# A fused attention and MLP training step: stage 1's weights in seven pieces, twelve tiles of the last stage loaded in the backward plan, the last block bank by bank

## The chip, the cores and the metric

The kernel runs on one core of a Trainium2 chip. The metric is the device time of one execution in microseconds (us). TensorE (PE in the profile) multiplies matrices into PSUM banks; VectorE (DVE) and ScalarE (ACT) evict and transform; GpSimd (POOL) copies small blocks and issues some DMAs; SyncE (SP) issues most DMAs. Each engine executes its own queue in order, and engines wait for each other and for DMAs by semaphores.

## The reference

The kernel computes the output of one layer and the gradients of all its ten inputs that are differentiated, for a sequence of 2048 rows of width 512, in bfloat16:

```
xn  = layernorm(x)
out = x + A(xn, mem0, Wq, Wk, Wv, Wo) + B(xn, w1, b1, w2, b2)

A:  64 segments of 32 rows, 32 heads of 128; the memory has 8 rows
    h   = concat(mem, xs)                    # 40 rows
    q, k, v = h @ Wq, h @ Wk, h @ Wv
    p   = softmax(mask(q k^T / sqrt(128)))
    o   = (p v) @ Wo
    mem = o[:8]; outs.append(o[8:])          # the next segment's memory
B:  relu(xn @ w1 + b1)^2 @ w2 + b2           # 512 -> 1792 -> 512

_out, _vjp = jax.vjp(_f, x, mem0, Wq, Wk, Wv, Wo, w1, b1, w2, b2)
return (_out, *_vjp(grad_out))
```

The memory makes the 64 segments a chain, forward and again backward.

## The kernel before

**Four parts follow each other.** Stage 1 (0 to about 230 us) does the layer norm, the MLP forward and its backward towards the input, for eight blocks of 256 rows. The forward chain (to about 1235 us) runs the 64 segments of the attention; the backward chain (to about 2264 us) runs them the other way, some 15 us each. The last stage (to the end) computes the gradients of Wv, Wk, Wq and Wo in 16 units of 160 matmuls each, with the rows of the layer norm's backward on VectorE beside them.

**The order of the work.** In the first three parts, operations are not issued where they are written: `A(cost, fn, reads, writes)` adds them to a `_Plan`, a list scheduler with modelled costs. `_Plan.run()` simulates the engines, picks by rank (the longest chain of costs behind an operation, plus hand-set biases from a table; stage 1 has none) and then issues everything in the order found. That order is fixed before the kernel runs; a DMA added or a cost changed can move other operations. `sg.dma` adds a DMA, on SyncE if nothing else is said (profile line L478), and names the keys that it reads and writes; a write waits for all earlier readers of the key. The last stage is written out by hand, in the order of its loops.

**Stage 1's start.** The loop over g (the row blocks) first loads the rows `xN[0]`, then by `CUT` the weights W1 and W2 in two pieces each, with the gradient's rows (`gxb`) and the bias (`b1Tb`) between them, then `b2r`. `ln(g)` normalises: ScalarE sums, VectorE subtracts the mean (L763), ScalarE squares, VectorE scales (L773), TensorE transposes to `ps_xT`, VectorE copies to `xT`. `turn_w` transposes weights on TensorE, two chunks of 128 columns at a time, into `W2T` and `W1T`. `mlp_a` (L796) makes for each of 14 chunks (fc) four matmuls with W1 against xT and four with W2T against gTb, then `r` (ScalarE, with the bias `b1T`, cast on VectorE at L894 from `b1Tb`), `aT` and `gh` (L803, VectorE). `gTb` is the transposed gradient: for block 0 it is made on TensorE, from block 1 on it is loaded by a transposing DMA (L746); `gb2p` (L806) sums it on VectorE. `mlp_b` multiplies aT with W2 and gh with W1T, seven chunks at a time.

**The end of the backward chain.** `chain(s)` takes one segment: for t = 2, 1, 0 (v, k, q) it makes `dN`, its transpose `dT` (L516), the products `ps_dRA` with the transposed weights (L1369), and stores `dN` to the DRAM tensor `S_GN[t]`. For the eight memory rows of four segments together `l_post` does the same: it loads `dLN` from `S_GNL`, transposes it to `LT0` and multiplies (`ps_dRL`, L1369). The transposed weights lie in `Wqkv[t]`; the key `((t, "WT"), n)` names a sixteenth of them. After the last segment `out2` is stored (`out_dram<-maskL`), `blk_out` copies `gNat` (shown as `maskL<-ps_gN`) and stores it in four pieces (`S_GOA<-maskL`).

**The last stage.** Unit x has a tensor t and a quarter j; it sums 20 row blocks (`NRC` = 16 + 4; `RCS` gives their order, y counts them) into eight PSUM banks. For t < 3 the left operand is a block of `HNc` (in the buffer WB) and the right one half of a tile `gbuf[y]`, 128x1024, 256 KB, loaded from `S_GN` or `S_GNL` (L1659 in `load_gn`). The tile buffers are, in this order: six in WB behind HNc, then the buffers `Wqkv[2]`, `Wqkv[1]`, `Wqkv[0]` as each becomes free (shown as WA), then some smaller ones. Already before, six tiles (`NEARLY`) of unit 0 are loaded in the plan, and their first four banks (24 matmuls, `mm0`, L1598) are planned too; the loop at L1688 does the rest. The first four banks are `pw0`. After a unit's matmuls the eight banks are evicted by ScalarE and VectorE in turn (`gwo`, L434 and L432), and stored from GpSimd's queue (L1699, L1701 for Wo).

Of the kernel before, what the change touches and what calls it, by code (L numbers as in the profile page):

```python
# [91 lines left out]
class _PE(dict):  # L92
    shape = None
    n = 8
# [213 lines left out]
def kernel(  # L308
# [27 lines left out]
    nc = tc.nc  # L336

    _, S, D = A_x.shape
    M = A_mem0.shape[1]
    H, Dh = A_Wq.shape[1], A_Wq.shape[2]  # L340
# [355 lines left out]
    with tc.tile_pool(name="p0", bufs=1) as p0, \  # L696
# [34 lines left out]
        gN0 = gxb[0][:].bitcast(BF16).rearrange("p (c d) -> p c d", c=2)  # L731
        CUT = ((0, 8), (8, FC))
        tiny = gb1[:, 0:1]
# [53 lines left out]
        def mlp_a(g):  # L787
            z = g % 2
            for fc in range(FC):
                bk = sg.bank("h", [P, 2, RB], F32, "ps_h")  # L790
                r = rT[fc % 2]
                rk = ("rT", fc % 2)
                for x, (Wt, wk, In, ik) in enumerate(((W1, ("W1", fc // 8), xT[z], ("xT", z)), (W2T, ("W2T", fc // 2), gTb[z], ("gT", z)))):
                    def mm(e, x=x, Wt=Wt, In=In, bk=bk, fc=fc):
                        for dc in range(DC):
                            nc.tensor.matmul(bk()[:, x, :], lhsT=Wt[:, dc, fc * P:(fc + 1) * P], rhs=In[:, dc, :],  # L796
                                             start=(dc == 0), stop=(dc == DC - 1), skip_group_check=True)
                    A({"PE": 0.44}, mm, [wk, ik], [bk] + ([("tick", g, fc)] if x else []))
# [12 lines left out]
        def mlp_b(g):  # L811
            z, y3 = g % 2, g % 3
            for rc in range(2):
# [6 lines left out]
                for bk, src, k, Wt, wk, first in ((bB, aT, "aT", W2, "W2", False), (bG, gh, "gh", W1T, "W1T", True)):  # L820
                    for q in range(2):
                        def mm(e, bk=bk, src=src, Wt=Wt, q=q, rc=rc, first=first):
                            for fc in range(7 * q, 7 * q + 7):
                                nc.tensor.matmul(bk()[:], lhsT=src[z][:, fc, rc * P:(rc + 1) * P], rhs=Wt[:, fc, :],
                                                 start=(fc == 0 and first), stop=(fc == FC - 1))
                        A({"PE": 1.52}, mm, [(wk, u) for u in (range(3 * q, 4 + 3 * q) if wk == "W1T" else range(q + 1))] + [(k, z, fc) for fc in range(7 * q, 7 * q + 7)], [bk])
                end = g == NRB - 1
# [9 lines left out]
        def turn_w(u, nm):  # L837
# [3 lines left out]
            def tr(e):  # L841
                for f in range(2):
                    for dc in range(DC):
                        if nm == "W1T":
                            transpose_to(bk()[:, DC * f + dc, :], W1[:, dc, (2 * u + f) * P:(2 * u + f + 1) * P])
                        else:
                            transpose_to(bk()[:, 2 * dc + f, :], W2[:, 2 * u + f, dc * P:(dc + 1) * P])
            A({"PE": 0.5}, tr, [(nm[:2], u // 4)], [bk])
            if nm == "W1T":
# [32 lines left out]
        for g in range(NRB):  # L882
            if g == 0:
                ln_in(0)
                for h, (f0, f1) in enumerate(CUT):
                    sg.dma(lambda f0=f0, f1=f1: W1[:, :, P * f0:P * f1],
                           lambda f0=f0, f1=f1: B_w1.rearrange("(c p) f -> p c f", p=P)[:, :, P * f0:P * f1], [], [("W1", h)], lat=6.0)
                    if h == 0:
                        sg.dma(lambda: gN0, lambda: pair(gflat, 0), [], ["gxb"], lat=6.0)
                        sg.dma(lambda: b1Tb[:], lambda: B_b1.rearrange("(c p) -> p c", p=P), [], ["b1Tb"], lat=5.0)  # L890
# [42 lines left out]
        for i in range(NI):  # L933
            sg.dma(lambda i=i: Wo[:, JQ * i:JQ * (i + 1), :].rearrange("p c d -> p (c d)"),
                   lambda i=i: A_Wo[JQ * i:JQ * (i + 1)].rearrange("j (a c) d -> (j a) (c d)", c=JQ),
                   (["WoL"] if i else []) + ([("gxo", 0), ("gxo", 1), ("S_B", TC - 2), ("S_B", TC - 1)] if i >= NI - 2 else []),
                   [] if i else ["WoL", ("W1", 0), ("W1", 1)] + [("W2T", u) for u in range(FC // 2)]
                   + [("xnN", w, k) for w in range(2) for k in range(2)],
# [359 lines left out]
    if True:  # L1298
# [278 lines left out]
        RCS = list(range(TC - 1, 0, -1)) + list(range(NRC - 1, TC, -1)) + [0, TC]  # L1577
        NEARLY = (H - NRC) * D // HW

# [5 lines left out]
        for x in range(NRC // BPC):  # L1585
# [5 lines left out]
            if x < 2:  # L1591
                for y in ((0, 1, 2), (3, 4, 5))[x]:
                    sg.dma(lambda y=y: gbuf[y], lambda y=y: gn_src(0, RCS[y]), ["HNw"], [("gn", y)], lat=3.5)
        pw0 = [sg.bank("w", [P, 512], F32, "ps_gw") for _ in range(4)]
        for y in range(NEARLY):
# [8 lines left out]
    with tc.tile_pool(name="p5b", bufs=1) as p5b, tc.tile_pool(name="p5e", bufs=1) as cs1, \  # L1604
# [60 lines left out]
        with tc.manual_schedule():  # L1665
            load_gn(0)
            for x in range(4 * JQ):
# [12 lines left out]
                kq = [(k % 4) * 2 + k // 4 for k in range(8)] if t < 3 else range(8)  # L1680
                for y in range(NRC):
                    rc = RCS[y]
                    for n, k in enumerate(kq):
                        if x == 0 and y < NEARLY and n < 4:
# [9 lines left out]
                for n, k in enumerate(kq):  # L1694
# [5 lines left out]
                    else:  # L1700
                        nc.gpsimd.dma_start(out_6[JQ * k + j], wt[:])  # L1701
                for z in lns:
# [38 lines left out]
```

## Time and profile before

| what | us |
|---|---|
| median of three runs | 2828.76 |
| the three runs | 2826.73, 2828.76, 2835.05 |
| the profiled execution, its own time | 2828.02 |
| its span | 2826.2 |
| TensorE busy | 2667.2 (94%) |
| VectorE busy | 1331.5 (47%) |
| ScalarE busy | 975.9 (35%) |
| GpSimd busy | 830.7 (29%) |
| mean granted clock of TensorE | 0.994 |

The span is the time from the first to the last record of the profiled execution; the execution itself was 1.8 us longer. A row of the timeline gives the start, the time, the engine, the line of the kernel, the operation, what it writes and reads, how many instructions are taken together, and in brackets the idle time before it with what ended it. "L1688" is line 1688 of the kernel before; helpers that record operations show their own line (L478 for DMAs, L432 and L434 for copies, L428 for transposes). The names of tiles are those of the program where they could be told; WA and WB are big shared buffers, and maskL is also used under other names.

### The profile page before, as it was taken

How to read it: one execution, taken by the hardware profiler on the slowest of the kernel's cores; microseconds unless marked ns; L12 is line 12 of the kernel's file. 1: busy time of each engine (PE TensorE's matmuls, PEld its weight loads, DVE VectorE, ACT ScalarE, POOL GpSimd, SP SyncE). 2: the span in 40 equal slices, each digit the busy share in tenths (PEclk: the TensorE clock that was granted, in tenths of full speed). 3: DMA queues.
4: the chain of work that ended last, by engine and by line, in shares of the span. 5: the costliest groups of instructions: out<-in, count | busy, mean ns of one | idle time of the engine just before them, and what ended most of it. 6: DMA issues, size and time to landing. Idle time of an engine off the chain costs nothing.

```text
span 2826.2 us, 125210 instructions
## 1 busy us (share of the span) xinstructions
PE 2667.2 (94%) x54888; PEld 1538.3 (54%) x55072; DVE 1331.5 (47%) x3344; ACT 975.9 (35%) x1995; POOL 830.7 (29%) x2439
## 2 busy tenths in 40 slices
PE   7998999999999999999999999999999899999998
PEld 5664555555555555575555555555555444444444
DVE  5554455555555555564545554545555402232321
ACT  4333444444444444453433444443334300000000
POOL 1111111111111111145555565555555301122211
PEclk9999999999999999999999999999999999999999
DMA  6657656556566666656776776677776698788860
GB/s 200 206 172 208 177 162 173 167 163 164 160 171 180 180 178 178 163 123 171 181 183 180 189 187 178 178 183 172 185 177 181 202 335 278 231 255 271 257 180 34
DMA packets 496306, 530.92 MB, mean 188 GB/s; under 512 B 223685, under 2 KB 321142, under 8 KB 493582
## 3 DMA queue, kind: packets, MB, share of 16 engines
q1 hardware_dynamic: 480318, 468.31, 59.8%
q0 software_dynamic: 15440, 54.61, 5.7%
q8 instruction: 430, 7.05, 1.1%
q14 instruction: 118, 0.97, 0.1%
HBM read 249.77 MB, written 237.52 MB: 172 GB/s over the span
## 4 chain that ended last, share of the span: by engine, by line
PE 37%; DMA 7%; issue 6%; DVE 3%; POOL 2%; ACT 1%; SPq 1%; POOLq 0%; DVEq 0%; ACTq 0%
PE ps_gw L1688 12%; PE ps_dRA L1369 11%; DMA S_R<-dT 5%; PE ps_dRL L1369 2%; PE ps_gO L537 2%; PE ps_d L623 2%; PE ps_d L598 1%; PE ps_d L572 1%; PE ps_gL L537 1%; PE ps_gOT L428 1%; PE ps_d L587 1%; DVE dT L516 1%; PE ps_dL L1480 1%; PE ps_gm L1523 1%; POOL out_dram L1701 1%
## 5 line engine op out<-in xcount | busy, mean ns | idle before, releaser
L1369 PE MATMUL ps_dRA<-WA,dT 128*32 128x512 bf16 x6144 | 374.5, 382 | 27.5 <-DVE dT L516 25.4
L1688 PE MATMUL ps_gw<-WA,WB 128*128 128x512 bf16 x1505 | 330.6, 379 | 1.6
L1688 PEld LDWEIGHTS <-WB 128*128 128x128 bf16 x1896 | 185.5, 98 | 229.4 <-DMA S_R<-dT 5.7
L537 PEld LDWEIGHTS <-PA 128*32 128x32 bf16 x8192 | 194.8, 96 | 195.7 <-DVE PA L1189 21.6
L434 ACT CAST dN<-ps_d 128x512 bf16<-128x512 f32 x356 | 199.2, 590 | 206.2 <-PE ps_d L598 109.3
L1369 PEld LDWEIGHTS <-dT 128*32 128x32 bf16 x6144 | 151.8, 96 | 178.6 <-DVE dT L516 46.1
L432 DVE CAST gwo<-ps_gw 128x512 bf16<-128x512 f32 x64 | 39.8, 684 | 400.8 <-PE ps_gw L1688 300.2
L516 DVE STREAM_TRANSPOSE dT<-dN 128x256 f32<-128x256 f32 x384 | 163.4, 435 | 115.3 <-ACT dN L434 55.7
L434 ACT CAST gwo<-ps_gw 128x512 bf16<-128x512 f32 x64 | 32.9, 599 | 515.6 <-PE ps_gw L1688 357.2
L1019 POOL TENSOR_TENSOR P<-P,rsA 128x320 bf16<-128x320 bf16 x64 | 46.1, 720 | 458.0 <-DVE rsA L1014 246.0
L610 POOL COPY BDP<-bP 32x256 bf16<-32x256 bf16 x256 | 101.2, 395 | 242.4 <-PE ps_d L572 234.2
L1699 POOL DMA_DIRECT2D out_dram<-gwo x96 | 71.4, 751 | 294.4 <-ACT gwo L434 264.6
L623 PEld LDWEIGHTS <-PB 32*32 32x32 bf16 x8192 | 118.5, 91 | 68.8 <-DVE PB L1167 22.3
L537 PE MATMUL ps_q<-WA,PA 128*32 128x512 bf16 x2048 | 144.5, 380 | 5.8 <-DVE PA L1189 4.0
L1038 PE MATMUL ps_RA<-WB,OT 128*32 128x256 bf16 x4096 | 129.5, 277 | 18.5 <-DVE OT L516 14.1
L537 PE MATMUL ps_k<-WA,PA 128*32 128x512 bf16 x2048 | 144.0, 379 | 0.3 <-DVE PA L1189 0.3
L537 PE MATMUL ps_v<-WA,PA 128*32 128x512 bf16 x2048 | 140.6, 379 | 0.0
L434 ACT CAST kN<-ps_k 128x512 bf16<-128x512 f32 x125 | 73.2, 586 | 192.3 <-PE ps_k L537 165.3
L1038 PEld LDWEIGHTS <-OT 128*32 128x32 bf16 x4096 | 104.3, 98 | 47.2 <-DVE OT L516 31.8
L537 PE MATMUL ps_gO<-WB,PA 128*32 128x512 bf16 x2048 | 125.8, 380 | 3.9 <-DVE PA L1527 3.0
L432 DVE CAST qN<-ps_q 128x512 bf16<-128x512 f32 x62 | 42.9, 692 | 171.0 <-PE ps_q L537 171.0
L1253 PE MATMUL ps_dw<-sx,anT 128*128 128x512 bf16 x339 | 108.2, 384 | 6.2 <-DMA sx<-S_XN 2.4
(315 smaller groups left out, 5248.7 us busy)
## 6 DMA issues: line engine op xcount, KB each, us to landing
S_GN<-dN SPq DMA_DIRECT2D x192, 256.0 KB
WA<-S_GN SPq DMA_DIRECT2D x160, 256.0 KB
S_Q<-qN SPq DMA_DIRECT2D x64, 256.0 KB
S_K<-kN SPq DMA_DIRECT2D x64, 256.0 KB
S_V<-vN SPq DMA_DIRECT2D x64, 256.0 KB
S_ON<-oN SPq DMA_DIRECT2D x64, 256.0 KB
bkN<-S_K SPq DMA_DIRECT2D x64, 256.0 KB
bqN<-S_Q SPq DMA_DIRECT2D x64, 256.0 KB
```

The source lines that it names most:

```text
L432: nc.vector.tensor_copy(out, in_)
L434: nc.scalar.copy(out, in_)
L516: self.plan.add({"DVE": 0.445}, lambda e, half=half: nc.vector.transpose(words(dst, half).rearrange("p (i c r) -> p i c r", i=4, c=2), src ...
L537: nc.tensor.matmul(bk()[32 * j:32 * (j + 1), :], lhsT=win(dc), rhs=Wt(dc, c0), start=(dc == 0), stop=(dc == DC - 1), tile_position=(0, 32 ...
L610: f(q_(dst, j)[:, :, j, 0:c], q_(src_f(), j))
L623: nc.tensor.matmul(bk()[32 * j:32 * j + m, k * P:(k + 1) * P], lhsT=lf(j, i), rhs=rf(j, i), start=(k == 0 and x == 0), stop=(x == n - 1), ...
L1019: A({"POOL": 0.72}, lambda e: nc.gpsimd.tensor_tensor(out=Et[:], in0=Et[:], in1=bc, op=ALU.mult), ["rsA"], ["P40"], 1)
L1038: nc.tensor.matmul(bk()[32 * c:32 * (c + 1), :], lhsT=sg.rows(OTt, i, j), rhs=Wo[:, JQ * i + j, dh * DH:(dh + 1) * DH], start=(i == 0 and ...
L1253: nc.tensor.matmul(bks[x]()[:], lhsT=anT[x][:, c, :], rhs=sx[z][:], start=(c == 0), stop=(c == TC - 1))
L1369: nc.tensor.matmul(bk()[32 * j:32 * (j + 1), :], lhsT=sg.rows(XT, i, j), rhs=wtf(t, i, j), start=(first and i == 0), stop=(last and i == N ...
L1688: nc.tensor.matmul(bks[n](), lhsT=HNc[:, rc, dc * P:(dc + 1) * P], rhs=gns[y][:, hf * 512:(hf + 1) * 512], start=(y == 0), stop=(y == NRC ...
L1699: nc.gpsimd.dma_start(outWs[t][dc * P:(dc + 1) * P, 4 * hf:4 * hf + 4, j, :], wt[:].rearrange("p (i e) -> p i e", i=4))
```

## The change

- **Stage 1.** `CUT` has seven pieces of two chunks instead of two pieces of eight and six. A piece of W1 is 256 of its 1792 columns (rows of 512 bytes), a piece of W2 256 of its rows. Everything that waits for a weight waits for its own piece: `mlp_a` and the turns for one, `mlp_b` for four. The gradient's rows and the bias are requested after the second piece of W1. In the order that the plan finds, SyncE issues xN0, W2's pieces 0 to 2, gxb, W2's 3 and 4, W1's 0 and 1, W2's 5 and 6, xN1, b1Tb, W1's 2 to 6, the transposed gTb, b2r, xN2; before, it was xN0, W2's first piece, gxb, W2's second, W1's first, xN1, b1Tb, W1's second, gTb, b2r, xN2. On VectorE the cast of b1T moves from ahead of the first normalising (L773) to some instructions behind it, and the first W1T copy from ahead of the first gh to behind it.
- **The join.** `NEARLY` is 18 instead of 6. Twelve more tiles of unit 0 are loaded in the backward plan, into the buffer of the transposed Wv, with the key of the sixteenth that each overwrites, so that each waits for the last reader of it. 48 more matmuls (12 tiles, four banks) move from the last stage's loop into the plan. In the order that results, TensorE has behind the last `ps_gN` transposes the 24 matmuls of the first six tiles, the dRL of t = 0 and t = 2, three matmuls of the loop, the 48 new ones, the dRL of t = 1, then the rest of unit 0; before, the 24 stood behind the dRL of t = 2, 8 of them behind that of t = 1. On SyncE ten of the twelve loads stand behind the four S_GOA stores and ahead of the last load of dLN (t = 1), two behind it. In the last three segments some operations of the chain change places on TensorE; the segments before them are as they were.
- **The end.** The last unit (x = 15) runs through its banks one by one, 20 matmuls each, instead of through its tiles with eight banks each; its eight stores are issued from SyncE instead of GpSimd.

```diff
-        CUT = ((0, 8), (8, FC))
+        CUT = tuple((f, f + 2) for f in range(0, FC, 2))
...
-                for x, (Wt, wk, In, ik) in enumerate(((W1, ("W1", fc // 8), xT[z], ("xT", z)), (W2T, ("W2T", fc // 2), gTb[z], ("gT", z)))):
+                for x, (Wt, wk, In, ik) in enumerate(((W1, ("W1", fc // 2), xT[z], ("xT", z)), (W2T, ("W2T", fc // 2), gTb[z], ("gT", z)))):
...
-                        A({"PE": 1.52}, mm, [(wk, u) for u in (range(3 * q, 4 + 3 * q) if wk == "W1T" else range(q + 1))] + [(k, z, fc) for fc in range(7 * q, 7 * q + 7)], [bk])
+                        A({"PE": 1.52}, mm, [(wk, u) for u in (range(3 * q, 4 + 3 * q) if wk == "W1T" else range(3 * q, 4 + 3 * q))] + [(k, z, fc) for fc in range(7 * q, 7 * q + 7)], [bk])
...
-            A({"PE": 0.5}, tr, [(nm[:2], u // 4)], [bk])
+            A({"PE": 0.5}, tr, [(nm[:2], u)], [bk])
...
                 for h, (f0, f1) in enumerate(CUT):
                     sg.dma(lambda f0=f0, f1=f1: W1[:, :, P * f0:P * f1],
                            lambda f0=f0, f1=f1: B_w1.rearrange("(c p) f -> p c f", p=P)[:, :, P * f0:P * f1], [], [("W1", h)], lat=6.0)
-                    if h == 0:
+                    if h == 1:
                         sg.dma(lambda: gN0, lambda: pair(gflat, 0), [], ["gxb"], lat=6.0)
                         sg.dma(lambda: b1Tb[:], lambda: B_b1.rearrange("(c p) -> p c", p=P), [], ["b1Tb"], lat=5.0)
...
-                   [] if i else ["WoL", ("W1", 0), ("W1", 1)] + [("W2T", u) for u in range(FC // 2)]
+                   [] if i else ["WoL", *[("W1", x) for x in range(FC // 2)]] + [("W2T", u) for u in range(FC // 2)]
...
-        NEARLY = (H - NRC) * D // HW
+        NFREE = (H - NRC) * D // HW
+        NEARLY = NRC - 2
...
+        for y in range(NFREE, NEARLY):
+            sg.dma(lambda y=y: gbuf[y], lambda y=y: gn_src(0, RCS[y]), ["HNw"] if y == NFREE else [],
+                   [("gn", y), ((2, "WT"), 4 * ((y - NFREE) % 4) + (y - NFREE) // 4)], lat=3.5)
...
-                for y in range(NRC):
-                    rc = RCS[y]
-                    for n, k in enumerate(kq):
+                end = x == 4 * JQ - 1
+                pairs = [(y, n) for n in range(8) for y in range(NRC)] if end else [(y, n) for y in range(NRC) for n in range(8)]
+                for y, n in pairs:
+                        rc, k = RCS[y], kq[n]
                         if x == 0 and y < NEARLY and n < 4:
                             continue
...
-                        nc.gpsimd.dma_start(out_6[JQ * k + j], wt[:])
+                        (nc.sync if end else nc.gpsimd).dma_start(out_6[JQ * k + j], wt[:])
```

## The prediction

> **What bounds the kernel now.** I read the shares of the engines first, then the chain that ended last, then the timeline of the three places that the edits touch: the first 25 us, the join of the backward chain and the last stage near 2260 us, and the last 10 us.
>
> ```profile
> PE 2667.2 (94%) x54888; PEld 1538.3 (54%) x55072; DVE 1331.5 (47%) x3344; ACT 975.9 (35%) x1995; POOL 830.7 (29%) x2439
> PE 37%; DMA 7%; issue 6%; DVE 3%; POOL 2%; ACT 1%; SPq 1%; POOLq 0%; DVEq 0%; ACTq 0%
> L1688 PE MATMUL ps_gw<-WA,WB 128*128 128x512 bf16 x1505 | 330.6, 379 | 1.6
> ```
>
> TensorE is busy for 2667.2 of 2826.2 us, so only 159 us can be had from waits. The last stage's matmuls had 1.6 us of idle time before 1505 of them: inside that stage nothing is to be won, only at its two ends. Sixteen units of 160 matmuls follow each other 34.53 us apart, 0.216 us a matmul.
>
> The start, from the timelines of SyncE, VectorE and TensorE (start, time, engine, work, idle before it and what ended that):
>
> ```profile
> 3.96 1.49 SPq L478 DMA_DIRECT2D xN<-in_A_x_dram  x1
> 6.77 6.76 SPq L478 DMA_DIRECT2D WB<-in_B_w_dram  x1
> 13.57 1.34 SPq L746 DMA_TRANSPOSE gTb<-in_grad_out_dram  x1
> ...
> 15.84 0.17 DVE L894 CAST b1T<-b1Tb 128x14 f32<-128x14 bf16 x1 [7.89 <-DMA b1Tb<-in_B_b_dram]
> 24.73 0.42 DVE L803 SCALAR_TENSOR_TENSOR gh<-ps_h,rT 128x256 bf16<-128x256 f32 x1
> ...
> 16.32 0.61 PE L428 MATMUL ps_xT<-ident,WB 128*128 128x128 bf16 x4 [7.24 <-DVE WB L773]
> 22.05 1.04 PE L796 MATMUL ps_h<-PA,WB 128*128 128x256 bf16 x8
> ```
>
> VectorE stands for 7.89 us at the cast of the bias b1, whose load is late; the normalising of L773 is queued behind it, and TensorE's first xT transposes wait for that. The first MLP matmul starts at 22.05, the first gh at 24.73. From there to the end of stage 1 (about 230 us) TensorE is over 99% busy, so what the start gains is kept.
>
> The join (timeline, then the windows: busy us of PE, PEld, DVE, ACT, POOL, then granted clock, DMA share, GB/s):
>
> ```profile
> 2250.77 1.91 PE L1369 MATMUL ps_dRL<-WA,LT 128*32 128x512 bf16 x32
> 2257.95 1.01 PE L1688 MATMUL ps_gw<-WB 128*128 128x512 bf16 x2 [5.27 <-DMA S_R<-dT]
> 2260.29 0.43 DVE L432 COPY maskL<-ps_gN 128x512 bf16<-128x512 bf16 x1 [10.11 <-DMA out_dram<-maskL]
> 2261.28 3.20 PE L1369 MATMUL ps_dRL<-WA,LT 128*32 128x512 bf16 x32
> 2262.95 3.61 SPq L1659 DMA_DIRECT2D WA<-S_GN  x7
> ...
> 2255.00:2260.00 5.00, 1.01 (x2) 0.28 (x3) 0.00 (x0) 0.00 (x0) 0.00 (x0) 0.71 0.84 299
> 2260.00:2265.00 5.00, 4.07 (x35) 1.39 (x36) 1.10 (x3) 0.00 (x0) 0.00 (x0) 0.61 0.33 68
> ```
>
> TensorE idles for 5.27 us and the clock falls to half from 2257.11 to 2263.94 (the 32 dRL matmuls take 3.20 there, 1.91 at full clock). SyncE issues the 256 KB loads of the last stage only from 2262.95, behind the store of out2, the four S_GOA stores and a load of dLN. The first unit of the last stage then ends at about 2300.5.
>
> The end (timeline):
>
> ```profile
> 2817.07 2.05 ACT L434 CAST gwo<-ps_gw 128x512 bf16<-128x512 f32 x4 [32.48 <-PE ps_gw L1692]
> 2817.24 2.49 DVE L432 CAST gwo<-ps_gw 128x512 bf16<-128x512 f32 x4 [25.14 <-PE ps_gw L1692]
> 2817.95 1.07 POOL L1701 DMA_DIRECT2D out_dram<-gwo  x2 [25.01 <-ACT gwo L434]
> 2820.19 3.20 POOL L1701 DMA_DIRECT2D out_dram<-gwo  x6 [1.17 <-issue]
> ```
>
> The last matmul ends at 2818.5; eight evictions and eight stores come after or around it, POOL stalls for 1.17 us and takes 0.54 a store, and the span ends 7.7 us after the last matmul.
>
> **The change part by part.** The sum is made against the profiled run, 2828.02 us (span 2826.2), which is 0.74 under the median of 2828.76; I add that back.
>
> *Stage 1.* The bias cast is moved behind the normalising on VectorE, and ahead of xN1 (second row block) 0.52 MB less is loaded. At the 375 GB/s of the stretch from 4 to 12 us that is 1.4 us: xN1 lands at about 13.2 instead of 14.34, b1Tb at 14.9 instead of 15.81. After the cast VectorE still has a W2T copy (0.69), the gb2p reduction (1.22) and the xT copy (0.69) before the first MLP matmul, which so starts near 18.9, 3.1 earlier. What is late next: SyncE now issues five W1 pieces of 256 KB between b1Tb and the transposed load gTb, and VectorE has the reduction over gTb (1.21) queued ahead of the first gh. The DMA packets of 512 B (a W1 piece has such rows) took 30 ns in the mean: 512 of them over 16 engines are 0.96 us a piece, so the pieces land until 19.7 and gTb 0.9 later (as after W1b before), at 20.6, against 18.69. Adding 1.21 and some 0.7 of small instructions gives the first gh at 22.5, 2.2 earlier. Of that I take back 1.0 since a W1T turn and its copy (0.61 PE, 0.69 DVE), which stood ahead of the first gh, now come after it: **-1.2**. Ends: -2.7, when only the 3.1 less half a turn counts; +0.5, when each piece takes as long as SyncE held xN1's 256 descriptors (1.49 us), which puts gTb at 23.3 and gh at 25.2.
>
> The Trainium skill, page "DMA: Bandwidth & Descriptors", Specifications, gives 512 B as the least transfer for full line rate, so by it the short pieces would cost nothing extra. The trace has 50 ns in the mean for 1 KB packets: twice 30 would be 60, so 512 B is a little slower; by the rule gTb would land 0.8 earlier and this part give -2.0.
>
> *The seven-way dependences* (turns of W1 and W2, mlp_b) add waits on single pieces, all landed by 20; the MLP uses a piece per 2.1 us (16 matmuls). Wo's load waits for stage 1's end as before: 0. Ten more DMA issues of 0.45 us lie on SyncE, which then waits for gTb anyway.
>
> *Join.* The order on TensorE in the last three segments is changed a little (dRA of one tensor before or after d0): by rows of the neighbouring segments -1.0, +1.1, +1.4, while the 1.43 us that TensorE spends there in "issue" is taken up: dm0 +0.3, in a range of -1 to +2. Then 24 first matmuls of the last stage stand ahead of the dRL of t=0 and t=2 and wait for the tiles until about 2257.8, so TensorE works in a stretch where it idled. out2 still lands near 2260.2 and VectorE's maskL copy, queued behind it, still frees the transpose for dRL t=2, which runs from 2261.1 at full clock to 2263.0 (-1.3 for the clock). Twelve tile loads into Wv's buffer now go out after S_GOA, ten ahead of the last dLN load: the first should land near 2267.1 (before: 2267.88 with dLN ahead at 2267.16), then one per 0.67 us. So 48 matmuls run from 2267.2 to 2277.6 (0.216 each, tiles 0.67 against 0.86 of work), dRL t=1 to 2279.5, and 85 matmuls (18.35) to 2297.9: **-2.6** against 2300.5. The tiles of the next unit that lie in Wk's buffer must wait for dRL t=1 until 2279.5; they have 18 us, at 0.67 a tile. If the reordered chain keeps its +2 and the clock falls again, the end is +2; if the chain gains 1, -4.
>
> *Tail.* Bank by bank, seven of eight evictions and stores lie beside matmuls (20 matmuls, 4.3 us, a bank). After 2818.5 one eviction (0.68) ends at 2819.2; a quiet SyncE store of the same 128 KB took 0.32 to issue and 1.36 from issue to landing: it lands at about 2820.9, and the span ended 1.34 after the last landing: 2822.3, **-3.9**. Ends: -4.6 (ScalarE's 0.60 and no gap), -2.5 (POOL's 1.17 stall coming back on SyncE). Same-bank matmuls are 0.216 apart too (ps_B in stage 1), so the loop order costs nothing.
>
> Sum: 2828.02 - 1.2 - 2.6 - 3.9 = 2820.3; with the 0.74, **2821**.
>
> **The rivals.**
>
> A, all parts pay in full: -2.7, -4.0, -4.6 make -11.3: 2817.5. For it: each gain is read from an idle stretch. Against it: gTb is late in the new queue.
>
> B, slower: the short pieces clog SyncE's queue. Before, one W1 load of 512 descriptors held SyncE for 6.76 us; now five of them stand ahead of gTb, for which VectorE waits in order. It decides from 2.5 us a piece on (5 x 1.5 us late eats the 6.5 of the other two parts and 1.2 of its own). At 2.98 (twice xN1's 1.49) it gives 2829, at 6.76 each 2848; as the middle 2835. Against it: that hold ended at 13.53 when the load before it landed (13.64) while the DMA engines moved 370 GB/s, so it was room, not pace.
>
> C, the join gives nothing: TensorE idles from 2263.0 to 2267.2 before the first tile. The clock changed in steps of 3.41 us, so an idle stretch of 4.2 holds a whole step in (4.2 - 3.41) / 3.41, about a quarter, of the cases; then 3.41 us at half clock cost 1.7, and with +1 from the chain the join is about 0: 2824. The Trainium skill, page "TensorE: Matmul & The Clock Gate", Part 1, has this as a rule: half rate after an idle window of some 3.4 us, with windows that run free. The drop at 2257.11, 4.4 us into the idle time, agrees.
>
> D, the change does not do what it says at the tail: SyncE is behind with loads or stalls as POOL did, and the tail gives 1.5: 2823.5.
>
> **How the numbers follow.** A measurement of this kernel tells about 0.3% (8.5 us) from no change, so faster means under 2820.3 and slower over 2837.3. The sum as worked out: 0.42, its own range 2818 to 2824, and since 2821 is next to the bound, 0.19 of it counts as faster. A 0.26 (faster), C 0.16 and D 0.06 (the same), B 0.10 (half of it slower). Faster 0.45, same 0.50, slower 0.05. The range runs from 2814 (A, and two of the six clock drops of the trace, 1.7 each, gone) to 2830 (C with such drops more, B's mild end): what it leaves out is most of B and a little of A.
>
> **What would show it.** Right: b1T's cast no longer ends a 7.9 us wait, and the first gh stands at 22 to 23; the clock in 2255 to 2265 is 1.00 and the 32 dRL take 1.9; the first eviction of the last stage stands some 2.6 earlier against dm0; the span ends 3.5 to 4 after the last matmul. Wrong: SyncE held for over 2 us at each W1 piece and the first gh after 25; a half clock near 2265; a wait of TensorE for tiles in the second unit; the last store issued more than 0.5 after its eviction. What the three places do not show, clock drops elsewhere in the chains, would move the time by some 1.7 to 3.4 each.

## The result, and the profile after

The changed kernel is slower. Its median is 2847.6 us (2836.6 to 2853.0, nine runs), the kernel before beside it 2832.6 us (2826.1 to 2840.5); the ratio is 1.0053, with a 95% interval of 1.0035 to 1.0072. Timed a second time, on another occasion, the ratio was 1.0043 (1.0027 to 1.0059). That is 12 to 15 us slower, where 8 us faster was forecast.

Two of the three places came out as forecast. I line the two profiled executions up by landmarks of the traces, so that the long chains between the places stay out of the comparison. A segment of the backward chain opens with its `ps_gO` matmuls (gO); dm0 is the first matmul on `ps_dm` (L1531), which makes out2 at the end of the last segment.

| stretch | before | after | forecast |
|---|---|---|---|
| start to the first matmul of the first segment (ps_q) | 230.8 | 229.5 | -1.2 |
| first gO matmul of the fourth segment from the end to that of the last | 45.7 | 50.0 | about +0.3 |
| last segment's first gO to dm0 | 15.2 | 15.3 | 0 |
| dm0 to the first eviction of the last stage | 49.6 | 61.6 | -2.9 (the join -2.6 in all) |
| first eviction of the last stage to the last matmul | 519.4 | 519.4 | 0 |
| last matmul to the end | 7.74 | 3.47 | -3.9 |

The rest of the profiled span's difference (2850.7 against 2826.2) lies in the long chains, which varied by as much between executions of one kernel (below). So the loss is at the join. TensorE's timeline there, in the changed kernel:

```profile
2266.23 1.70 PE L1531 MATMUL ps_dm<-dT,sel 128*8 128x512 f32 x2 [0.93 <-DVE dT L432]
2267.87 0.61 PE L428 MATMUL ps_gN<-ident,PA 128*128 128x128 bf16 x4
2272.96 2.29 PE L1602 MATMUL ps_gw<-WB 128*128 128x512 bf16 x5 [4.49 <-DMA S_RL<-btL]
2275.48 4.65 PE L1602 MATMUL ps_gw<-WB 128*128 128x512 bf16 x18 [0.22 <-issue]
2280.06 3.64 PE L1369 MATMUL ps_dRL<-WA,LT 128*32 128x512 bf16 x64
2283.86 0.59 PE L1693 MATMUL ps_gw<-WB 128*128 128x512 bf16 x2 [0.16 <-issue]
2294.62 13.23 PE L1602 MATMUL ps_gw<-WA,WB 128*128 128x512 bf16 x47 [10.17 <-DMA WA<-S_GN]
```

Before the 48 new matmuls TensorE idles for 10.17 us, and waits for a tile load. Most of the loads are not that late, as SyncE's timeline shows:

```profile
2276.91 1.70 SPq L478 DMA_DIRECT2D S_GOA<-maskL  x4
2282.45 2.24 SPq L478 DMA_DIRECT2D WA<-S_GN  x5
2284.74 1.37 SPq L478 DMA_DIRECT2D WA<-S_GNL  x3
2286.16 0.90 SPq L478 DMA_DIRECT2D WA<-S_GN  x2
2287.16 0.38 SPq L478 DMA_DIRECT2D dLN<-S_GNL  x1
2287.58 1.12 SPq L478 DMA_DIRECT2D WA<-S_GN  x2
```

The first of the twelve (issued at 2282.45) landed at 2285.06, the last (issued at 2288.05) at 2294.58, and TensorE starts 0.04 after the last landing. The order hints at why: three loads from S_GNL stand sixth to eighth, but those are the tiles 15, 16 and 17, the last to be used. The windows of that stretch (columns as in the windows of before) show the second price: the clock stands at half in 2290 to 2300, and the 47 matmuls take 0.28 us each instead of 0.216.

```profile
2270.00:2275.00 5.00, 2.04 (x5) 0.72 (x6) 0.00 (x0) 0.00 (x0) 0.00 (x0) 0.50 0.95 288
2285.00:2290.00 5.00, 0.00 (x0) 0.00 (x0) 0.00 (x0) 0.00 (x0) 0.00 (x0) 0.69 0.99 349
2290.00:2295.00 5.00, 0.38 (x2) 0.11 (x2) 0.77 (x2) 0.00 (x0) 0.00 (x0) 0.50 1.03 344
2295.00:2300.00 5.00, 5.00 (x13) 1.76 (x12) 0.00 (x0) 0.00 (x0) 0.00 (x0) 0.50 0.31 118
```

**Where the order comes from.** The planner's hand-set biases are a list per part of the program, handed out by position. The list `l_post` has 40 entries: 23 for l_post itself, 11 for the loads of the last stage, 6 for the six groups of four matmuls (`mm0`). The change puts twelve loads between the 11 and the six groups. So the last six entries (-138.8, 4, 60.5, -26.2, -46, -16.4), meant for the groups, now go to the loads of the tiles 6 to 11, and the groups have none. Tile 6, with -138.8, is loaded last of the twelve (14, 7, 8, 12, 13, 15, 16, 17, 11, 9, 10, 6). The groups lose the -138.8 that kept them behind dRL and move ahead of it. And since the groups are chained by their banks, eighteen of them instead of six give everything that stands ahead of them a higher rank (+10.3), which reorders the last three segments.

The start, VectorE's timeline of the changed kernel:

```profile
16.52 0.17 DVE L894 CAST b1T<-b1Tb 128x14 f32<-128x14 bf16 x1
...
21.58 1.22 DVE L806 TENSOR_REDUCE gb2p<-gTb 128x4 f32<-128x1024 bf16 x1 [1.59 <-DMA gTb<-in_grad_out_dram]
...
23.24 0.41 DVE L803 SCALAR_TENSOR_TENSOR gh<-ps_h,rT 128x256 bf16<-128x256 f32 x1
```

The bias cast ends no wait any more, gTb is the next thing late (1.59 us of waiting), and the first gh comes at 23.24 instead of 24.73. The end, from the timeline:

```profile
2844.04 3.19 PE L1697 MATMUL ps_gw<-GOc,WA 128*128 128x512 bf16 x13
2847.26 0.69 DVE L432 CAST gwo<-ps_gw 128x512 bf16<-128x512 f32 x1 [7.94 <-PE ps_gw L1697]
2847.98 0.33 SPq L1706 DMA_DIRECT2D out_dram<-gwo  x1
```

One eviction and one store are left after the last matmul.

### The profile page after: what moved, and what is told of

It is laid out like the page before. It is cut to its first block, busy times and chain, and to the rows that moved or that the text cites. A ratio compares the mean times of both kernels' runs of the same rounds, so it can differ in the third digit from the quotient of the medians.

```text
span 2850.7 us, 125218 instructions
## 1 busy us (share of the span) xinstructions
PE 2677.9 (94%) x54887; PEld 1540.5 (54%) x55072; DVE 1333.4 (47%) x3343; ACT 978.1 (34%) x1996; POOL 830.2 (29%) x2431
## 4 chain that ended last, share of the span: by engine, by line
PE 44%; DMA 6%; DVE 3%; POOL 2%; issue 1%; SPq 1%; ACT 1%; DVEq 0%; POOLq 0%; ACTq 0%
PE ps_gw L1693 14%; PE ps_dRA L1369 10%; PE ps_gw L1697 5%; DMA S_R<-dT 4%; PE ps_gO L537 2%; PE ps_dRL L1369 2%; PE ps_d L623 2%; PE ps_d L572 1%; PE ps_d L598 1%; PE ps_gL L537 1%; PE ps_gOT L428 1%; PE ps_d L587 1%; DMA dLN<-S_GNL 1%; PE ps_gw L1602 1%; SPq L478 1%
## 5 line engine op out<-in xcount | busy, mean ns | idle before, releaser
L1693 PE MATMUL ps_gw<-WA,WB 128*128 128x512 bf16 x1459 | 320.4, 379 | 1.5
```

Of the source, the lines that this page charges most:

```text
L1693: nc.tensor.matmul(bks[n](), lhsT=HNc[:, rc, dc * P:(dc + 1) * P], rhs=gns[y][:, hf * 512:(hf + 1) * 512], start=(y == 0), stop=(y == NRC ...
```

## The experiments

The theory: the whole loss is one of order, made by the shifted biases and ranks; loading the tiles early and moving the 48 matmuls costs nothing by itself. The first rival: the loads crowd the DMA engines, or must wait for the transposed weights, whatever their order. A second: the new stage 1 lengthens the forward chain, which was 7.6 us longer in the first profile (1011.9 us from ps_q to the first gO of the backward chain, 1004.3 before).

**The tiles in the order of use, all else as in the changed kernel.** Each of the twelve loads keeps its place, but takes the next tile that will be used:

```diff
+        nexty = iter(range(NFREE, NEARLY))
+
+        def load_next(e):
+            y = next(nexty)
+            nc.sync.dma_start(gbuf[y], gn_src(0, RCS[y]))
         for y in range(NFREE, NEARLY):
-            sg.dma(lambda y=y: gbuf[y], lambda y=y: gn_src(0, RCS[y]), ["HNw"] if y == NFREE else [],
-                   [("gn", y), ((2, "WT"), 4 * ((y - NFREE) % 4) + (y - NFREE) // 4)], lat=3.5)
+            A({"SP": T_DMA}, load_next, ["HNw"] if y == NFREE else [],
+              [("gn", y), ((2, "WT"), 4 * ((y - NFREE) % 4) + (y - NFREE) // 4)], 1, 3.5)
```

> The changed kernel with one thing mended: the twelve new tile loads keep their places in every queue, but fetch the tiles in the order in which TensorE uses them (6, 7, ... 17) instead of 14, 7, 8, 12, 13, 15, 16, 17, 11, 9, 10, 6. Theory 1 (TensorE's first new matmul waits for the tile that is loaded last): the idle time before the new matmuls falls from 10.2 us to about 1, the clock stays up, and the 48 matmuls take about 10.4 us instead of 13.2; the kernel is 11 to 13 us faster than the changed one, about 2835 where the changed one has 2847. Rival (the loads crowd the DMA engines or wait for the transposed weights, whatever their order): the idle time stays above 7 us and the time within 4 us of the changed kernel's.

Measured: 2827.8 us, before 2828.5, ratio 1.0000 (0.9988 to 1.0012). TensorE's timeline:

```profile
2258.58 1.02 PE L1531 MATMUL ps_dm<-dT,sel 128*8 128x512 f32 x2 [0.94 <-DVE dT L432]
2266.42 2.29 PE L1607 MATMUL ps_gw<-WB 128*128 128x512 bf16 x5 [6.49 <-DMA S_RL<-btL]
...
2277.36 0.59 PE L1698 MATMUL ps_gw<-WB 128*128 128x512 bf16 x2 [0.16 <-issue]
2278.56 1.89 PE L1607 MATMUL ps_gw<-WA,WB 128*128 128x512 bf16 x8 [0.60 <-DMA WA<-S_GN]
2280.97 8.93 PE L1607 MATMUL ps_gw<-WA,WB 128*128 128x512 bf16 x39 [0.52 <-DMA WA<-S_GN]
```

The wait of 10.17 us is 0.60 now, the matmuls run at full clock, and from dm0 to the first eviction it is 51.3 us instead of 61.6. The order of the loads alone is worth 10.3 us: the largest part of the loss. The first rival falls, since the same loads in the same places now cost next to nothing (51.3, where seven profiles with the old join have 50.6 in the mean).

**The order of before kept.** The loads take no biases and a low rank, the six groups get their biases back, and the new groups do not raise the ranks ahead of them:

```diff
+        at, plan.at = plan.at, len(plan.bias)
         for y in range(NFREE, NEARLY):
-            sg.dma(lambda y=y: gbuf[y], ...)
+            plan.add({"SP": T_DMA}, lambda e, y=y: nc.sync.dma_start(gbuf[y], gn_src(0, RCS[y])), ...
+                     lift=-60.0 + (10.32 if y == NFREE else 0.0))
+        plan.at = at
...
-            A(pe(0.86, "f", 4), mm0, [("gn", y), ("HN", RCS[y] // BPC), "gNat"], pw0)
+            A(pe(0.86, "f", 4), mm0, [("gn", y), ("HN", RCS[y] // BPC), "gNat"], pw0, lift=-10.32 if y == NFREE else 0.0)
```

> The changed kernel, but the twelve loads take no entries of the table of biases (the six matmul groups of before get theirs back), have a low rank, and the new matmul groups do not raise the rank of what stands before them: so the order of the backward plan is that of before on all engines up to its last few operations, and the tiles come in the order of use. Theory 1 (all of the loss at the join comes from the shifted biases and ranks, that is from the order of the tiles, the 24 matmuls ahead of dRL and the changed order in the last three segments): the loss of some 19 us at the join turns into a gain of 0 to 3, and the whole is at 2825 to 2830 where before has 2832. Rival (loading the twelve tiles and moving 48 matmuls costs by itself, for example by waiting for dRL of t = 2 or by crowding the DMA engines): at least 5 us slower than before at the join, 2834 or more in all.

Measured: 2828.1 us, before 2828.5, ratio 0.9996 (0.9983 to 1.0009). The loss at the join is gone: 47.5 us over the last three segments, 50.0 from dm0 to the first eviction. But there is no gain either, which my forecast had as 2.6: with the matmuls behind dRL, TensorE works almost without a gap from dRL of t = 2 on, both in this kernel and in the kernel before, and the idle stretch ahead of it is as it was.

**The join alone.** The changed kernel with the edits of stage 1 and of the last block undone, so that against before only this is left:

```diff
-        NEARLY = (H - NRC) * D // HW
+        NFREE = (H - NRC) * D // HW
+        NEARLY = NRC - 2
...
+        for y in range(NFREE, NEARLY):
+            sg.dma(lambda y=y: gbuf[y], lambda y=y: gn_src(0, RCS[y]), ["HNw"] if y == NFREE else [],
...
```

> The kernel before with the second part of the change alone (the twelve loads and 48 matmuls in the backward plan). Theory 1: it carries the whole loss and some more, 17 to 21 us slower than before, with the first eviction of the last stage 60 us or more after dm0 instead of 50. Rival (the loss comes in part from the forward chain, which was 6 us longer in the profiled run of the changed kernel, by way of stage 1's new pieces): at most 12 us slower than before.

Measured: 2840.9 us, before 2828.5, ratio 1.0049 (1.0031 to 1.0068). From dm0 to the first eviction 62.3 us. About 14 us of loss, less than the 17 to 21 expected, but no less than the whole change's 12 to 15.

**Stage 1 and the last block, without the join.** Against the changed kernel:

```diff
-        NFREE = (H - NRC) * D // HW
-        NEARLY = NRC - 2
+        NEARLY = (H - NRC) * D // HW
...
-        for y in range(NFREE, NEARLY):
-            sg.dma(lambda y=y: gbuf[y], lambda y=y: gn_src(0, RCS[y]), ["HNw"] if y == NFREE else [],
...
```

> The kernel before with the first and third part of the change (seven pieces; last block bank by bank, stored from SyncE), without the join. Theory 1: the tail gives 4 us, stage 1 about nothing (0 to -1), the chains are unchanged: 3 to 6 us faster than before. Rival (stage 1's new pieces lengthen stage 1 or the forward chain): as fast as before or slower.

Measured: 2824.4 us, before 2828.5, ratio 0.9994 (0.9978 to 1.0009). The sign is as expected, but the interval holds both theories. In the profile ps_q starts at 229.5, and the end is 3.47 after the last matmul.

**The changed kernel again**, beside the next three:

> The changed kernel once more, beside the kernels below. The sum of the places seen so far (stage 1 -1.7, last three segments +2.6, from dm0 to the first eviction +12, tail -4.2) gives 9 us slower than before. If instead the forward chain, which was 6 us longer in its first profile, is slower by itself, the run is 14 us or more slower and its forward chain is again at least 5 us longer than before's.

Measured: 2840.5 us, before 2825.4, ratio 1.0043 (1.0027 to 1.0059). In this profile the forward chain took 1003.5 us, as in the kernel before, and from dm0 to the first eviction it was 60.9: the chain's extra time in the first profile was not the change's.

**All loads in the order of use.** The six first tiles and the five loads of HNc (HN 0 to 4, four row blocks each) were out of order too (tiles 4, 5, 1, 3, 2, 0). Now the eleven places fetch by use:

```diff
+        turns = iter([("HN", 3), ("gn", 0), ("gn", 1), ("gn", 2), ("gn", 3), ("HN", 2), ("gn", 4), ("gn", 5),
+                      ("HN", 1), ("HN", 0), ("HN", 4)])
+        def load_turn(e):
+            kind, x = next(turns)
...
-                    sg.dma(lambda y=y: gbuf[y], lambda y=y: gn_src(0, RCS[y]), ["HNw"], [("gn", y)], lat=3.5)
+                    A({"SP": T_DMA}, load_turn, ["HNw"], [("gn", y)], 1, 3.5)
```

> As the changed kernel with the twelve tiles in the order of use; now the first eleven loads of the last stage (six tiles and five blocks of HNc) also keep their places on SyncE but fetch in the order of use: HN 3, tiles 0 to 3, HN 2, tiles 4 and 5, HN 1, 0, 4. Theory 1 (the 24 matmuls placed ahead of dRL wait for tile 0, which is loaded last of the six): they start within 1.5 us of ps_gN instead of 6.5 us later, fill the idle stretch at full clock, and dm0 to the first eviction falls from 51.3 to about 47.5; 3 to 4 us faster than with the twelve alone, about 2824 where before has 2828.5. Rival (the load of dLN, the store of out2 and the copy behind it set the end of dRL whatever TensorE does in between): dm0 to the first eviction stays at 50 to 51 and the time too.

Measured: 2822.4 us, before 2825.4, ratio 0.9990 (0.9974 to 1.0006). The timeline of TensorE:

```profile
2250.37 1.03 PE L1531 MATMUL ps_dm<-dT,sel 128*8 128x512 f32 x2 [0.61 <-DVE dT L432]
2251.32 0.40 PE L428 MATMUL ps_gN<-ident,PA 128*128 128x128 bf16 x4
2251.56 5.34 PE L1616 MATMUL ps_gw<-WB 128*128 128x512 bf16 x24
2256.83 1.91 PE L1369 MATMUL ps_dRL<-WA,LT 128*32 128x512 bf16 x32
2262.73 2.92 PE L1369 MATMUL ps_dRL<-WA,LT 128*32 128x512 bf16 x32 [3.99 <-DVE LT L516]
```

The 24 matmuls now fill the idle stretch, as I had forecast for the change itself, and from dm0 to the first eviction it is 47.7 us, 3.6 less. That is the 2.9 below the old join's mean of 50.6 that was forecast, but not by the forecast's route: dRL of t = 2 still ends 15.3 us after dm0 (15.0 before), and the gain is that the 24 matmuls are done by then. What is left is the wait of 3.99 us ahead of dRL of t = 2.

**Three loads of HNc later, so that dLN comes earlier.** In the kernel just shown, the loads of HN 1, 0 and 4 get a low rank:

```diff
-            A({"SP": T_DMA}, load_turn, ["HNw"] if x else [], [("HN", c0 // BPC)] + ([] if x else ["WB", "HNw"]), 1, 4.0)
+            A({"SP": T_DMA}, load_turn, ["HNw"] if x else [], [("HN", c0 // BPC)] + ([] if x else ["WB", "HNw"]), 1, 4.0,
+              lift=-200.0 if x > 1 else 0.0)
```

> As the kernel above, with three of the five HNc loads (512 KB each) moved on SyncE behind the load of dLN for t = 2; every other engine's order is that of the changed kernel. If the load of dLN is late because 1.5 MB stand ahead of it (the DMA engines move some 390 GB/s there), it lands about 4 us earlier against dm0, dRL of t = 2 follows earlier, and dm0 to the first eviction falls by 2 to 4 more, to 44 or 46. If out2's store and the copy behind it, or the store of eL before dLN, set it, nothing changes.

Measured: 2826.9 us, before 2825.4, ratio 0.9999 (0.9984 to 1.0014). dLN did land earlier, 4.3 us after dm0 instead of 8.6, and nothing came of it: 47.6 us from dm0 to the first eviction. The rival named there, that out2's store and the copy behind it set the time, is tested next.

**out2 staged apart**, on top of that:

```diff
-                sg.evict(lambda: gNat[0:M, :], bm, lambda: bm()[:], ["gNat"], 0, EV_F)
-                sg.dma(lambda: out2flat[:, :], lambda: gNat[0:M, :], ["gNat"], [])
+                om = VT[0:M].rearrange("p i j k -> p (i j k)")[:, 0:D]
+                sg.evict(lambda: om, bm, lambda: bm()[:], ["gNat"], 0, EV_F)
+                sg.dma(lambda: out2flat[:, :], lambda: om, ["gNat"], [])
```

> As the kernel with the late HNc loads (all orders the same), but the 8 rows of out2 are staged in a tile of their own (the buffer of the transposed values, which is free by then) instead of in the first rows of gNat. If the store of out2 is what holds VectorE's copy of gNat and the LT transposes queued behind it, VectorE no longer waits 11.5 us there, dRL of t = 2 follows dRL of t = 0 without the 3 to 4 us of idle time, and dm0 to the first eviction falls from 47.6 to about 44.5. Rival (the load of dLN sets it, or the tile loads behind it do): 47 or more.

Measured: 2833.6 us, before 2837.6, ratio 0.9992 (0.9979 to 1.0006). VectorE's timeline, first of the kernel with all loads in the order of use, then of this one:

```profile
2261.90 0.42 DVE L432 COPY maskL<-ps_gN 128x512 bf16<-128x512 bf16 x1 [11.59 <-DMA out_dram<-maskL]
2262.24 0.76 DVE L516 STREAM_TRANSPOSE LT<-dLN 128x256 f32<-128x256 f32 x2
```

```profile
2260.39 0.42 DVE L432 COPY maskL<-ps_gN 128x512 bf16<-128x512 bf16 x1 [2.51 <-DMA S_GN<-dN]
2267.13 0.45 DVE L516 STREAM_TRANSPOSE LT<-dLN 128x256 f32<-128x256 f32 x1 [6.32 <-PE ps_dRL L1369]
```

The copy no longer waits for the store of out2, the transposes now wait for TensorE, and from dm0 to the first eviction it is 44.1 us, 3.5 less again and 6.5 below the mean of the old join. So it was out2's store that held the copy; the time as a whole is not clearly below before's.

**The chain's order.** First the changed kernel with the biases right but the raised ranks left:

```diff
+        at, plan.at = plan.at, len(plan.bias)
         for y in range(NFREE, NEARLY):
             sg.dma(lambda y=y: gbuf[y], lambda y=y: gn_src(0, RCS[y]), ["HNw"] if y == NFREE else [],
                    [("gn", y), ((2, "WT"), 4 * ((y - NFREE) % 4) + (y - NFREE) // 4)], lat=3.5)
+        plan.at = at
```

> The changed kernel, where the twelve loads take no entries of the table of biases and the first six matmul groups get theirs back: the tiles come in the order of use and the 24 matmuls stand behind dRL again; only the ranks ahead of the join stay raised by the longer chain of matmul groups. From dm0 to the first eviction 50 as before (the 24 ahead of dRL cost some 1.3 in the kernel with the tiles alone in order), while the last but one segment still takes 19 to 20 us instead of 15 if the raised ranks make it so; with 15 it was the biases.

Measured: 2840.3 us, before 2837.6, ratio 1.0014 (0.9998 to 1.0029); 50.5 us from dm0 to the first eviction, and 19.4 for the last but one segment. So the long segment comes from the raised ranks, not from the shifted biases.

Then a kernel with everything found so far, and with ranks set so that TensorE's order up to dm0 is that of before. The last l_post is entered behind the first six groups and waits for them, which puts the 24 matmuls ahead of dRL:

```diff
-        l_post(0)
         NRC = TC + NLC
+        plan.scope("l_post")
+        plan.at = 23
...
+            if y == NFREE:
+                l_post(0)
+                plan.at = len(plan.bias)
...
-            A(pe(0.86, "f", 4), mm0, [("gn", y), ("HN", RCS[y] // BPC), "gNat"], pw0)
+            A(pe(0.86, "f", 4), mm0, [("gn", y), ("HN", RCS[y] // BPC), "gNat"], pw0 + (["early"] if y == NFREE - 1 else []),
+              lift=-17.47 if y == NFREE - 1 else 0.0)
...
-                bR = dh_part("l" if b else LKIND, ..., [] if b else ["gNat"])
+                bR = dh_part("l" if b else LKIND, ..., [] if b else ["gNat", "early"])
```

> All findings in one kernel: stage 1 and the tail as changed, the loads of the last stage in the order of use, out2 staged apart, and ranks set so that TensorE's order up to dm0 is that of the kernel before, with the 24 matmuls of the first six tiles behind ps_gN. Stage 1 -1.7, last three segments 0 (45.7 to 48.4 as before, with 15 us from the last but one to the last instead of 20), dm0 to the first eviction -5, tail -4.2: about 11 us faster than before, ratio 0.996. If the chain's order was not what made the last but one segment 20 us long, it stays at 19 to 20 and the gain is about 8.

Measured: 2836.3 us, before 2837.6, ratio 0.9994 (0.9976 to 1.0013). TensorE's order up to dm0 is that of before, and the last but one segment is 15.3 us again (15.2 in the kernel with the order of before kept), so the order made it 20. But the whole stayed short of the 11 us expected, in part at the join: the load of dLN is now issued behind the S_R store, 4.5 us after dm0, and the transposes wait for it, in VectorE's timeline of this kernel:

```profile
2278.62 0.77 DVE L516 STREAM_TRANSPOSE LT<-dLN 128x256 f32<-128x256 f32 x2 [9.70 <-DMA dLN<-S_GNL]
```

So from dm0 to the first eviction it is 48.0, 2.6 below the mean of the old join where 5 were expected. The rest of the shortfall is not explained by this.

What the changed order costs in the last but one segment can be read in part in VectorE's timeline, first of the kernel before, then of the changed one:

```profile
2233.89 0.19 DVE L1527 CAST PA<-ps_gm 128x32 bf16<-128x32 f32 x1 [0.44 <-PE ps_gm L1523]
```

```profile
2250.32 0.45 DVE L516 STREAM_TRANSPOSE LT<-dLN 128x256 f32<-128x256 f32 x1 [2.98 <-DMA dLN<-S_GNL]
2250.69 0.15 DVE L1527 CAST PA<-ps_gm 128x32 bf16<-128x32 f32 x1
```

The small copy of ps_gm, which the next segment's gO needs, is now queued behind a transpose that waits 2.98 us for a load, and TensorE idles for 2.31 us ahead of gO. That is about half of the 4.9 us that this segment lost: TensorE idled for 4.2 us in it in all (0.6 before) and was busy for 1.3 more, which is not told apart further.

**Stage 1 alone, and the spread.** The parts read from the profiles add up to 8.7 us of loss, and several kernels with the new stage 1 came out some 4 us over the sum of their parts. So I timed stage 1's edits alone, twice, beside two copies of the kernel before, and the last block's edits alone (each part's lines of the diff shown with the change, nothing else):

> The kernel before with stage 1's pieces alone. By the profiles its first segment's matmuls start 1.7 us earlier; from there every engine's order is that of before. If the parts add up, 1 to 2 us faster than before, ratio 0.9994. If the new pieces cost something later on that the places looked at do not show, 2 to 4 us slower, ratio 1.001, as the sums over the kernels run so far suggest (those with the new pieces came out some 4 us over the sum of their parts, the two without them did not).

> The same kernel once more, for a second profile and a second interval. Same numbers as for the first, whichever theory holds; if the two differ by more than 3 us, the difference looked for is below what such runs can tell.

> The kernel before, unchanged, for the spread of its chains: the forward chain took 1001.5 to 1004.3 us in the three profiles with the old stage 1 and 1002.5 to 1011.9 in the ten with the new one. If the chains' length varies by the phase of the clock's windows alone, this profile may lie anywhere in 1001 to 1012, and its ratio to before is 1.000 within 0.0015. If the new pieces lengthen the chain, it lies in 1001 to 1005.

> As the copy above, for another profile: ratio 1.000 within 0.0015; forward chain 1001 to 1005 if stage 1's pieces matter for it, anywhere up to 1012 if the phase of the clock's windows sets it.

> The kernel before with the third part alone. The span ends 3.5 us after the last matmul instead of 7.7, as in the changed kernel's profile, and the time is 3 to 5 us below before's, near the limit of what five rounds tell. If the last block's eviction had been hidden by something, or SyncE were behind, the end would stay above 6 us.

Measured: stage 1 alone 0.9990 (0.9970 to 1.0009) and 0.9993 (0.9973 to 1.0013); the copies of before 1.0006 (0.9989 to 1.0022) and 0.9995 (0.9975 to 1.0014); the last block alone 0.9986 (0.9969 to 1.0002), with 3.60 us after the last matmul. The suspicion against stage 1 is not borne out: alone it is, if anything, a little faster, and a copy of the kernel before took 1011.4 us from ps_q to the first gO of the backward chain, where others with the old stage 1 took 1001.5 to 1004.3. It is not ruled out either: the second interval reaches 1.0013, and the forward chain took 1007.3 us in the mean of twelve profiles with the new pieces, 1004.8 in five with the old, with spreads of 9 to 10 us in both.

## Why the prediction was wrong

- **Stage 1: right in size, in part by luck.** Forecast -1.2; ps_q starts at 229.4 in the mean of twelve profiles with the new pieces (228.7 to 230.5) against 230.7 in five with the old (230.1 to 231.1): -1.3. The first MLP matmul stood at 19.06 where I had 18.9, and gTb became the next wait. But the steps behind these numbers were off both ways: xN1 landed at 14.40, not at 13.2 (before: 14.34), b1Tb at 15.68, not at 14.9, and the last W1 piece and gTb at 20.59 and 21.56, 0.9 and 1.0 later than forecast. So the first gh came at 23.24 instead of 22.5, 1.5 earlier than before instead of 2.2, and of the 1.0 that I took back only 0.2 was lost. Rival B, a clogged queue, did not come: SyncE issued the five late pieces in 6.24 us, 1.25 each, under the 2.5 from which it would have decided. (By its own rule of five pieces its prices would have been 1 to 2 us higher than the 2829 and 2848 that I gave.)
- **Tail: right.** Forecast -3.9, measured 7.74 to 3.47, -4.3. The eviction took 0.69 us where I had 0.68, the store's issue 0.33 where I had 0.32.
- **Join: wrong, and this decided the sign.** The step that failed is "the first should land near 2267.1 ... then one per 0.67 us. So 48 matmuls run from 2267.2". I had the order of the loads on SyncE by number and size, but not by tile, and took it for the order of use. The loads did land one per 0.8 us from 2.6 us after the first issue, where I had one per 0.67; but tile 6, the first one needed, came last, 9.5 us after the first landing. With the half clock behind the wait this is 10.3 of the 11.0 us that the stretch from dm0 lost (61.6 in the mean of three profiles, against 50.6 in seven with the old join).
- **A second error in the same step.** I let the 24 matmuls wait for tiles until about 2257.8 and still had the 64 dRL done at 2263.0. The 24 take 5.2 us and the 64 another 3.8, so by my own numbers dRL could not end before 2266.8. In the changed kernel the matmuls started 6.7 us after dm0 and dRL of t = 2 ended 17.5 us after it, 15.0 before. The tile loads wait for that dRL.
- **The chain: mis-sized.** Forecast "dm0 +0.3, in a range of -1 to +2"; the last three segments took 50.1 us in the mean of seven profiles with the new order, 46.8 in seven with the old: +3.3. The step added up shifts of TensorE's instructions, and missed, among other things, that a copy on VectorE came to stand behind a transpose that waits for a load (2.31 us of TensorE's idle time).
- **Rival C** named the right place, but with half a window of the clock as its price (1.7 us) and a wait of 4.2 us; the wait was 10.2. None of the rivals had an end at 2848 by way of the join, and the range ended at 2830.
- The Trainium skill's rule on the clock (page "TensorE: Matmul & The Clock Gate", Part 1: half rate after an idle window of some 3.4 us) held in part: within a trace all falls of the clock lie at the same phase of a 3.41 us grid, as it says, but a window need not be idle. In the changed kernel the clock falls at 2266.45 us, ahead of the wait of 4.49 us, after a window in which TensorE was busy for 1.62 of 3.41 us, and at 2286.93 after one with 0.81. So my estimate of a quarter for rival C was too low.
- The Trainium skill's 512 B as the least transfer for full line rate (page "DMA: Bandwidth & Descriptors", Specifications) was not borne out by the packets: from 9.8 to 21.6 us of the changed kernel, packets of 512 B took 31.0 ns in the mean (16.5 bytes a ns) and packets of 1 KB 51.5 ns (19.9). gTb was waited for until 21.58, 1.0 us later than the row's pace of 30 ns had it and 1.8 later than the rule. The transposing load itself held SyncE for 2.73 us (1.34 before), so not all of this lateness need come from the pieces.

**What stays open.** The parts give +3.3 and +11.0, less 1.3 and 4.3: 8.7 us slower, where 15 (10 to 20) and 12 (8 to 17) were measured. The sum lies within the second interval, and just outside the first. For the kernel with out2 apart the parts give some 9 us of gain (-1.3 + 3.3 - 6.5 - 4.3), measured were 2 (0.9979 to 1.0006, so at most 6). Stage 1 and the last block together gave 2, where their parts give 5.6 (the interval, 0.9978 to 1.0009, still holds that). The chains between the places vary: in two profiles of the changed kernel the forward chain took 1011.9 and 1003.5 us, the backward chain up to the fourth segment from its end 959.5 and 947.6. The 17 profiles have between 24 and 55 us of half clock in these two stretches, and of three profiles of the kernel before, the one with 34 us of it in the forward chain took 1011.4, those with 17 and 21 took 1004.3 and 1003.1. Why the kernels with all the gains did not show them in full isn't settled. No kernel here was shown to beat the kernel before; the ones that come nearest are the last block alone (0.9986) and all loads in the order of use (0.9990), with intervals that just reach 1.

## What to carry to other kernels

When a change adds operations to a planned order, list not only how many of them stand where, but which: compare the order in which loads are issued with the order in which they are used, item by item, because an engine that works in order waits for the first one needed, however early the others are. Tables that are handed out by position shift when something is put in the middle; a change "about loads" then reorders matmuls as well. And work that is moved into an idle stretch gains only if its own inputs are there by then, and delays everything behind it on its engine if they are not.

## What the runs showed of the hardware

- A wait of 10.17 us cost 13.2 us: TensorE's 47 matmuls behind it took 0.28 us each in the mean, since the clock stood at half for 13.65 us from 2286.93.
- The clock falls after a window that is half idle, not only after an idle one. I cut the 17 traces into windows of 3.41 us at each trace's own phase, from 30 us to the end of the last unit but one, and took those at full clock, some 13,500. 168 were followed by half clock: all in which TensorE was busy under 40% of the window were among them, none over 60%; between, it went either way. In only 19 of the 168 was TensorE busy for less than 1%. Two such windows of the changed kernel, with the columns of the windows above:

```profile
2263.01:2266.42 3.41, 1.62 (x21) 0.43 (x17) 0.42 (x1) 0.37 (x1) 0.00 (x0) 1.00 1.06 372
2283.48:2286.89 3.41, 0.81 (x7) 0.31 (x4) 0.00 (x0) 0.00 (x0) 0.00 (x0) 1.00 0.97 332
```

- The phase of these windows is another in each execution (0.9, 0.0, 0.4, 0.3, 0.6, 1.3, 2.1 us in the first seven profiles), so the same waits of a segment can fall into one window or be shared by two. Runs of one kernel on one chip differed by up to 27 us (35 runs of the kernel before, 2814.2 to 2841.2); that the phase makes this spread was not tried.
- Two kernels of the same order, one with a 4.3 us earlier load of dLN, took the same time (47.7 and 47.6 us at the join), because a store of 8 KB, queued behind loads of 256 and 512 KB, took 7.0 and 6.3 us from issue to landing and held a copy that overwrites its source; with out2 staged apart it was 44.1. The 32 KB stores of the changed kernel's S_GOA, with no load ahead of them, took 1.5.
